# A long convolution and two MLP layers on one core: the work that GpSimd did behind the filter's first layer goes to VectorE

## The chip, the cores and the metric

The kernel runs on one core of a Trainium2 chip. The metric is device time in microseconds (us), measured around the whole program. The kernel before takes 1390.85 us, the median of three runs that lie between 1390.0 and 1391.01 us.

A core has five engines with a queue each: TensorE (PE, with the weight loads PEld beside it), VectorE (DVE), ScalarE (ACT), GpSimd (POOL) and SyncE (SP, here only for DMAs). An engine takes its instructions in the order of its queue. Matmul results land in PSUM; a tile of PSUM or SBUF that is used again has to be free first, and that is a wait as much as a missing operand is.

## The reference

```
h    = (relu(pos_emb @ w1) @ w2) * exp(-0.01*pos)      # filter, S=12480 x 128
y    = irfft(rfft(x*v, 2S) * rfft(h, 2S))[:S]          # long convolution
a    = x * y                                           # 12480 x 128
r    = relu(a @ moe_w_in)**2 @ moe_w_out               # 128 -> 2048 -> 128
h2   = r @ moe2_w_in
out  = (h2 * sigmoid(1.702*h2)) @ moe2_w_out           # 128 -> 2048 -> 128
```

All in fp32. The four weight matrices of the MLP come as 64-bit floats, which the kernel reads as pairs of 32-bit words (`raw`, low and high word side by side) and turns into two fp32r parts each, `hi` (rounded) and `lo` (the rest); each matmul of the MLP is three: hi*hi, hi*lo, lo*hi.

## The kernel before

**Stages.** The convolution is a Fourier transform of length 99 x 127 in two stages and back. Until 22 us the filter's first layer runs, until 87 us the first transform stage. From 87 to 227 us, `stage_s2` handles 99 frequencies in 50 pairs p: for each pair TensorE makes the spectrum `xk`, and of every fourth frequency on the filter's features `fk` and its spectrum `hk`; ScalarE copies `hk` to `hc`; VectorE makes the four partial products `t` (L357) of the complex product and the real half of `P` (L361, 128x256), GpSimd the imaginary half (L360); TensorE transforms back to `ob` (L369), ScalarE copies it into `A` (L371), and a DMA per four frequencies writes `A` to `bd` in DRAM. At the end the first columns of `bd` are read back transposed into `A` (`load_first`, L458).

**The boundary.** Between `stage_s2` and the MLP, `work.finish()` ends the weight conversions of the first MLP layer, and `sums_first` adds and subtracts halves of what was read back into `Gs` (L433 on VectorE, six times). With them TensorE makes tile 0 of the convolution's result (`yps`, L516); VectorE multiplies by x (L504 to L506, `hi`, `y`, `lo`). While it waits, TensorE repeats a matmul whose result nobody reads (`spare`, L645).

**The MLP.** 25 tiles of about 500 positions, 8 units a tile and layer. A unit is six matmuls in (`hin`) and, four units later (LAG), six out (`acc`). Layer 1 of the MLP on ACT: Relu (L588), Square (L589), and for every third of the first 40 units the rounding to `gh` (L591); on DVE that rounding else (L601, `gate`) and `gl = g - gh` (L612, `low`). The first 40 units (tiles 0 to 4) belong to layer 1 alone; from then on units of both layers alternate. For each later tile the sums of two rows of `bd` (`combine`, L433: 126 in all, 99x256) were GpSimd's, and so was a narrow rest of `y` (L532). The order per step n of the main loop: `work.tick(n)`, `unit_out` of n-4, `unit_in` of n, `high` of n-1, `gate` of n, `low` of n-1, then what the tile's own step brings: the loads at j=0, `front_rest` after j=2 of tile 0, `front_y` of the next tile after j=3, `front_x` after j=5.

**Weight conversions.** A chunk is 128x512 weights. `conversion` is a generator of ten steps; each tick advances it by one. Seven VectorE operations (L135 to L148) build the number in `cs` and `cm`, one tick each; then ScalarE rounds it to `hi` (L150), a tick without work, and VectorE makes `lo` (L152). Chunks 0 to 7 are done in `stage_s2` and `finish`, chunks 8 to 15 in the MLP from n=3 on, one every six steps.

**Names.** `uv` are rows of `bd` as loaded for sums, `b` and `Gs` hold sums, `yps` is the PSUM tile of the convolution's result, `yr` the kept rest columns, `xs` the columns of x.

Of the kernel before, what the change touches and what calls it, by code (L numbers as in the profile page):

```python
# [95 lines left out]
def conv_mlp_kernel(ctx: ExitStack, tc: tile.TileContext, xc, xt, vc, pt, w1, w2,  # L96
# [8 lines left out]
    ci2 = const.tile([N1, 2, N1], FP32, name="ci2")  # L105

# [18 lines left out]
    def conversion(n, raw, pool):  # L125
# [33 lines left out]
    class Weights:  # L159
# [60 lines left out]
    def filter_stage(fp, bank, h, inputs):  # L220
# [6 lines left out]
        nc.vector.memset(warm, 0.0)  # L227
        p_t = {}
# [76 lines left out]
    def stage_s2(sp, mp, A, w2b, hooks, work):  # L305
# [9 lines left out]
        with kp as kp, obp as obp:  # L315
# [14 lines left out]
            def filters(g):  # L330
# [10 lines left out]
                h_c[g] = sp.tile([128, FK, 2, D], FP32, tag="hc", name="hc", bufs=3)  # L341
# [39 lines left out]
            for p in range(NP + 2):  # L381
# [467 lines left out]
```

## Time and profile before

| | |
|---|---|
| median of three runs | 1390.85 us |
| the profiled execution | 1392.53 us, of which the span is 1390.7 us |
| TensorE busy in the span | 1377.2 us, 99% |
| VectorE, ScalarE, GpSimd busy | 1104.7, 949.6, 208.9 us |
| granted TensorE clock, mean | 0.998 of full speed |

How it is read: the span starts with the first and ends with the last instruction. A row of a timeline gives the start, the time that the row's instructions took together, engine, line, operation, output and inputs, and in brackets how long the engine sat idle before it and what ended that. [...] A row of a group by line gives the count, the busy time and the mean of one in ns, then the idle time before.

### The profile page before, as it was taken

How to read it: one execution, taken by the hardware profiler on the slowest of the kernel's cores; microseconds unless marked ns; L12 is line 12 of the kernel's file. 1: busy time of each engine (PE TensorE's matmuls, PEld its weight loads, DVE VectorE, ACT ScalarE, POOL GpSimd, SP SyncE). 2: the span in 40 equal slices, each digit the busy share in tenths (PEclk: the TensorE clock that was granted, in tenths of full speed). 3: DMA queues.
4: the chain of work that ended last, by engine and by line, in shares of the span. 5: the costliest groups of instructions: out<-in, count | busy, mean ns of one | idle time of the engine just before them, and what ended most of it. 6: DMA issues, size and time to landing. Idle time of an engine off the chain costs nothing.

```text
span 1390.7 us, 19236 instructions
## 1 busy us (share of the span) xinstructions
PE 1377.2 (99%) x7756; PEld 1143.1 (82%) x7756; DVE 1104.7 (79%) x1170; ACT 949.6 (68%) x1071; POOL 208.9 (15%) x208
## 2 busy tenths in 40 slices
PE   9999998999999999999999999999999999999998
PEld 8888885878788888888888888888888888888887
DVE  7559997888997777778777877777777777778887
ACT  2655553888776776667677776777677766777776
POOL 3013333522221011201121011111110120000000
PEclk9999999999999999999999999999999999999999
DMA  9967785212100001000010000100000100000000
GB/s 261 307 215 265 269 266 178 77 50 69 47 20 27 25 10 32 27 27 9 20 39 27 8 27 20 39 9 27 20 27 8 39 19 9 8 8 8 8 15 15
DMA packets 46583, 89.67 MB, mean 64 GB/s; under 512 B 4221, under 2 KB 31038, under 8 KB 45982
## 3 DMA queue, kind: packets, MB, share of 16 engines
q1 hardware_dynamic: 37427, 63.69, 15.1%
q10 hardware_dynamic: 9067, 24.75, 4.7%
q8 instruction: 61, 1.00, 0.3%
q14 instruction: 28, 0.23, 0.0%
HBM read 63.62 MB, written 24.81 MB: 64 GB/s over the span
## 4 chain that ended last, share of the span: by engine, by line
PE 79%; DVE 2%; ACT 2%; issue 0%; ACTq 0%
PE acc L560 13%; PE hin L560 13%; PE hin L561 13%; PE acc L561 13%; PE hin L562 12%; PE acc L562 12%; PE yps L516 3%; DVE gl L612 1%; ACT g L589 1%; ACT g L588 1%; DVE gh L601 0%; DVE g L603 0%; ACT gh L591 0%; DVE lo L493 0%; PE hin L578 0%
## 5 line engine op out<-in xcount | busy, mean ns | idle before, releaser
L612 DVE TENSOR_TENSOR gl<-g,gh 128x1004 fp32r<-128x1004 f32 (+4 forms) x400 | 493.6, 1234 | 33.8 <-ACT gh L608 33.6
L588 ACT ACTIVATE g<-hin 128x1004 f32<-128x1004 f32 (+4 forms) x200 | 201.1, 1005 | 226.9 <-PE hin L562 214.5
L560 PE MATMUL acc<-gh,w 128*128 128x502 f32 (+4 forms) x800 | 314.0, 392 | 2.4 <-DVE lo L493 2.4
L561 PE MATMUL acc<-gl,w 128*128 128x502 f32 (+4 forms) x800 | 312.1, 390 | 1.3 <-DVE gl L612 1.2
L562 PE MATMUL acc<-gh,w 128*128 128x502 f32 (+4 forms) x800 | 311.6, 390 | 0.0
L560 PE MATMUL hin<-hi,w 128*128 128x502 f32 (+4 forms) x798 | 311.3, 390 | 0.3 <-DVE g L603 0.3
L561 PE MATMUL hin<-lo,w 128*128 128x502 f32 (+4 forms) x798 | 311.0, 390 | 0.0
L562 PE MATMUL hin<-hi,w 128*128 128x502 f32 (+4 forms) x798 | 310.5, 389 | 0.0
L603 DVE TENSOR_TENSOR g<-hin,g 128x1004 f32<-128x1004 f32 (+4 forms) x200 | 238.6, 1193 | 46.6 <-ACT g L593 46.4
L601 DVE CAST gh<-g 128x1004 fp32r<-128x1004 f32 (+4 forms) x185 | 132.8, 718 | 152.0 <-ACT g L589 152.0
L593 ACT ACTIVATE g<-hin 128x1004 f32<-128x1004 f32 (+4 forms) x200 | 200.0, 1000 | 73.8 <-PE hin L562 65.8
L589 ACT ACTIVATE g<-g 128x1004 f32<-128x1004 f32 (+4 forms) x200 | 208.0, 1040 | 6.3
L608 ACT CAST gh<-g 128x1004 fp32r<-128x1004 f32 (+4 forms) x200 | 202.7, 1014 | 1.7 <-DVE g L603 1.7
L560 PEld LDWEIGHTS acc<-gh,w 128*128 128x128 f32 x800 | 150.9, 189 | 35.6 <-DVE lo L493 2.8
L560 PEld LDWEIGHTS hin<-hi,w 128*128 128x128 f32 x798 | 150.5, 189 | 34.8 <-ACT g L588 2.1
L561 PEld LDWEIGHTS acc<-gl,w 128*128 128x128 f32 x800 | 150.7, 188 | 31.9 <-DVE gl L612 2.5
L562 PEld LDWEIGHTS acc<-gh,w 128*128 128x128 f32 x800 | 150.7, 188 | 30.7
L562 PEld LDWEIGHTS hin<-hi,w 128*128 128x128 f32 x798 | 150.8, 189 | 30.4
L561 PEld LDWEIGHTS hin<-lo,w 128*128 128x128 f32 x798 | 150.9, 189 | 29.9
L433 POOL TENSOR_TENSOR Gs<-uv 99x256 f32<-99x256 f32 x82 | 91.8, 1149 | 442.2 <-DMA uv<-bd 367.2
L433 POOL TENSOR_TENSOR b<-uv 99x256 f32<-99x256 f32 x44 | 48.9, 1140 | 269.9 <-DMA uv<-bd 194.8
L360 POOL TENSOR_TENSOR P<-t 128x256 f32<-128x256 f32 (+1 forms) x50 | 48.1, 961 | 155.6 <-DVE t L357 139.2
(72 smaller groups left out, 1047.2 us busy)
## 6 DMA issues: line engine op xcount, KB each, us to landing
uv<-bd SPq DMA_DIRECT2D x64, 198.0 KB
m<-in_c_s_dram SPq DMA_DIRECT2D x49, 256.0 KB
bd<-A ACTq DMA_DIRECT2D x24, 512.0 KB
x<-in_xc_dram SPq DMA_DIRECT2D x16, 384.0 KB
v<-in_vc_dram SPq DMA_DIRECT2D x16, 384.0 KB
Gs<-gd ACTq DMA_DIRECT2D x10, 512.0 KB
raw<-in_moe_w_in_dram SPq DMA_DIRECT2D x8, 512.0 KB
raw<-in_moe_w_out_dram SPq DMA_DIRECT2D x8, 512.0 KB
```

The lines of the kernel that those rows point to most:

```text
L360: nc.gpsimd.tensor_tensor(out=P[:, 0:n, 1], in0=t[:, 0:n, 0, 1], in1=t[:, 0:n, 1, 0], op=ALU.add)
L433: engine.tensor_tensor(out=b[:, :, s, c], in0=uv[:, 0, :, c], in1=uv[:, 1, :, 1 - c], op=ALU.add if s != c else ALU.subtract)
L560: nc.tensor.matmul(out=out, lhsT=a, rhs=hl[0], start=first, stop=False)
L561: nc.tensor.matmul(out=out, lhsT=a, rhs=hl[1], start=False, stop=False)
L562: nc.tensor.matmul(out=out, lhsT=b, rhs=hl[0], start=False, stop=last)
L588: nc.scalar.activation(out=g, in_=ps, func=ACTF.Relu)
L589: nc.scalar.activation(out=g, in_=g, func=ACTF.Square)
L593: nc.scalar.activation(out=g, in_=ps, func=ACTF.Sigmoid, scale=1.702)
L601: nc.vector.tensor_copy(out=gh, in_=g)
L603: nc.vector.tensor_tensor(out=g, in0=ps, in1=g, op=ALU.mult)
L608: nc.scalar.copy(out=gh, in_=g)
L612: nc.vector.tensor_tensor(out=gl, in0=g, in1=gh.bitcast(FP32), op=ALU.subtract)
```

## The change

GpSimd keeps only the sums of the filter's first layer. In `stage_s2` the filter's spectrum is stored with a negated copy of its imaginary part in front (one more ScalarE operation for each group, L351), so that one VectorE operation on 128x512 (L370) makes both halves of `P`. The last pair but one writes to another PSUM tile, the last result is copied by VectorE, `hk` of the last group moves ahead by two steps, and both reads of `bd` at the end go through SyncE's queue. The conversions write into the raw words instead of a tile `cs`, in six steps; in `stage_s2` two of the eight VectorE operations become ScalarE activations; all eight chunks run there, from step 2 every six steps. In a conversion the last two VectorE operations and ScalarE's copy (L157) now come in one tick. In the MLP a `combine_two` (L455 or L457, 99x512) takes the place of two `combine`; the sums of a tile wait in a list, `pending`, and VectorE takes two off it at each of j=1, 2 and 3 of a unit of layer 1, ahead of `gate`. The conversions there start at n=4.

```diff
@@ conversion
-        yield vec.tensor_scalar(out=s, in0=high, scalar1=20, scalar2=0x7FF, ...)
-        yield vec.tensor_scalar(out=s, in0=s, scalar1=896.0, scalar2=1151.0, op0=ALU.max, op1=ALU.min)
-        yield vec.tensor_scalar(out=s, in0=s, scalar1=896.0, scalar2=float(1 << 23), ...)
-        yield vec.scalar_tensor_tensor(out=s, in0=high, scalar=-(1 << 31), in1=s, ...)
-        m = pool.tile([128, WC], I32, tag="cm", name="cm", bufs=2)
+        m = pool.tile([128, WC], I32, tag="cm", name="cm", bufs=1)
         f = m.bitcast(FP32)
-        yield vec.tensor_scalar(out=m, in0=high, ...)
+        vec.tensor_scalar(out=m, in0=high, ...)
         yield vec.scalar_tensor_tensor(out=f, in0=low.bitcast(U32), scalar=2.0 ** -32, in1=m, ...)
-        yield vec.scalar_tensor_tensor(out=f, in0=f, scalar=2.0 ** -20, in1=s.bitcast(FP32), ...)
+        vec.tensor_scalar(out=low, in0=high, scalar1=20, scalar2=0x7FF, ...)
+        if i < 2:
+            nc.scalar.activation(out=low.bitcast(FP32), in_=low, func=ACTF.Relu,
+                                 scale=-1.0, bias=edges[:, 0:1])
+            yield nc.scalar.activation(out=low, in_=low.bitcast(FP32), func=ACTF.Relu,
+                                       scale=-float(1 << 23), bias=edges[:, 1:2])
+            yield
+        else:
+            yield vec.tensor_scalar(out=low, in0=low, scalar1=896.0, scalar2=1151.0, ...)
+            yield vec.tensor_scalar(out=low, in0=low, scalar1=896.0, scalar2=float(1 << 23), ...)
+        vec.scalar_tensor_tensor(out=low, in0=high, scalar=-(1 << 31), in1=low, ...)
+        vec.scalar_tensor_tensor(out=f, in0=f, scalar=2.0 ** -20, in1=low.bitcast(FP32), ...)
         yield nc.scalar.copy(out=hi, in_=f)
         yield
         yield vec.tensor_tensor(out=lo, in0=f, in1=hi.bitcast(FP32), op=ALU.subtract)
@@ filters, product, back
-                nc.scalar.copy(out=h_c[g][:, 0:n], in_=hk[:, :, 0:n].rearrange("p c k d -> p k c d"))
+                nc.scalar.copy(out=hc[:, 0:n, 1:3], in_=hk[:, :, 0:n].rearrange("p c k d -> p k c d"))
+                nc.scalar.activation(out=hc[:, 0:n, 0], in_=hk[:, 1, 0:n], func=ACTF.Copy, scale=-1.0)
...
-                nc.gpsimd.tensor_tensor(out=P[:, 0:n, 1], in0=t[:, 0:n, 0, 1], in1=t[:, 0:n, 1, 0], op=ALU.add)
-                nc.vector.tensor_tensor(out=P[:, 0:n, 0], in0=t[:, 0:n, 0, 0], in1=t[:, 0:n, 1, 1],
-                                        op=ALU.subtract)
+                nc.vector.tensor_tensor(out=P[:, 0:n], in0=t[:, 0:n, 0], in1=t[:, 0:n, 1], op=ALU.add)
...
-                nc.scalar.copy(out=A[:, 2 * p:2 * p + n], in_=ob[:, 0:n])
+                (nc.vector.tensor_copy if p == NP - 1 else nc.scalar.copy)(
+                    out=A[:, 2 * p:2 * p + n], in_=ob[:, 0:n])
@@ stage_s2
-                if p < NP - 2:
+                if p < NP - 4:
                     work.tick(p)
@@ combine
+    def combine_two(k, op):
+        uv, b = b_t[k]
+        b = b.rearrange("n j s c d -> n j (s c) d")
+        u, v = uv[:, 0], uv[:, 1]
+        if op == ALU.add:
+            nc.vector.tensor_tensor(out=b[:, :, 1:3], in0=u[:, :, ::-1], in1=v, op=op)
+        else:
+            nc.vector.tensor_tensor(out=b[:, :, 0:4:3], in0=u, in1=v[:, :, ::-1], op=op)
+    def pend(k):
+        pending.extend((k, op) for op in (ALU.add, ALU.subtract))
+    def combine_next(n):
+        for i in range(min(n, len(pending))):
+            combine_two(*pending.pop(0))
@@ load_b, load_rest
-            for s in range(1 if k < KF else 2):
-                for c in range(2):
-                    combine(k, s, c, nc.gpsimd)
+            pend(k)
@@ front_y
-                nc.gpsimd.tensor_tensor(out=y[:, n:], in0=yr[:, at:at + m], in1=x[:, n:n + m], op=ALU.mult)
+                nc.vector.tensor_tensor(out=y[:, n:], in0=yr[:, at:at + m], in1=x[:, n:n + m], op=ALU.mult)
@@ main loop of the MLP
-        spare(8)
+        spare(6)
...
-        work = Weights([8, 12, 9, 13, 10, 14, 11, 15], 3, 6, 3, cp)
+        work = Weights([8, 12, 9, 13, 10, 14, 11, 15], 4, 6, 3, cp)
...
                 if prev:
                     high(prev)
+                if l == 0 and j in (1, 2, 3):
+                    combine_next(2)
                 gate(un)
@@ conversions of the first layer
-            work = Weights([0, 4, 1, 5, 2, 6, 3], 3, 6.5, 5, cp, [(46, 7)])
+            work = Weights([0, 4, 1, 5, 2, 6, 3, 7], 2, 6, 5, cp)
```

VectorE's queue from the last product of `stage_s2` to the first result of tile 0, before (`w0` is a weight tile, `cs` and `cm` the conversions' tiles):

```order
L357 TENSOR_TENSOR t_2229<-xk_2213,hc_2200 128x512
L361 TENSOR_TENSOR P_2231<-t_2229 128x128
L148 SCALAR_TENSOR_TENSOR cm_2172<-cm_2172,cs_2077 128x512
L135 TENSOR_SCALAR cs_2250<-raw_2174 128x512
L137 TENSOR_SCALAR cs_2250<-cs_2250 128x512
L138 TENSOR_SCALAR cs_2250<-cs_2250 128x512
L152 TENSOR_TENSOR w0_958<-cm_2172,w0_958 128x512
L140 SCALAR_TENSOR_TENSOR cs_2250<-raw_2174,cs_2250 128x512
L144 TENSOR_SCALAR cm_2257<-raw_2174 128x512
...
L433 TENSOR_TENSOR Gs_69<-A_535 99x2x128 x6
L504 TENSOR_TENSOR hi0_2327<-yps_2306,xs_2136 128x492
```

The same stretch after:

```order
L367 TENSOR_TENSOR t_2210<-xk_2195,hc_2159 128x512
L370 TENSOR_TENSOR P_2212<-t_2210 128x256
L381 COPY A_538<-ob_2214 128x256
L153 SCALAR_TENSOR_TENSOR raw_1990<-raw_1990 128x512
L155 SCALAR_TENSOR_TENSOR cm_2121<-cm_2121,raw_1990 128x512
L159 TENSOR_TENSOR w0_961<-cm_2121,w0_961 128x512
L455 TENSOR_TENSOR Gs_70<-A_538 99x2x256
L457 TENSOR_TENSOR Gs_70<-A_538 99x2x2x128
L446 TENSOR_TENSOR Gs_70<-A_538 99x2x128 x2
L534 TENSOR_TENSOR hi0_2293<-yps_2272,xs_2124 128x492
```

Ten operations of conversions stood between the last product and the sums (three are left out above); three stand there now, and the copy of the last `ob` ahead of them.

VectorE's queue in tile 0, before (numbers tell the tiles apart: `gl_2354` is unit 0, `gl_2381` unit 1):

```order
L601 CAST gh_2353<-g_2352 128x2x492
L612 TENSOR_TENSOR gl_2354<-g_2352,gh_2353 128x2x492
L601 CAST gh_2394<-g_2393 128x2x492
L612 TENSOR_TENSOR gl_2381<-g_2379,gh_2380 128x2x492
L552 COPY yr_2296<-yps_2400 128x196
```

And after (`uv_2301` are the rest's rows, `uv_2320` and `uv_2323` those for tile 1):

```order
L629 CAST gh_2313<-g_2312 128x2x492
L455 TENSOR_TENSOR b_2304<-uv_2301 99x2x256
L457 TENSOR_TENSOR b_2304<-uv_2301 99x2x2x128
L640 TENSOR_TENSOR gl_2314<-g_2312,gh_2313 128x2x492
L455 TENSOR_TENSOR Gs_70<-uv_2320 99x2x256
L457 TENSOR_TENSOR Gs_70<-uv_2320 99x2x2x128
L629 CAST gh_2352<-g_2351 128x2x492
L640 TENSOR_TENSOR gl_2337<-g_2335,gh_2336 128x2x492
L580 COPY yr_2264<-yps_2360 128x196
L455 TENSOR_TENSOR Gs_70<-uv_2323 99x2x256
L457 TENSOR_TENSOR Gs_70<-uv_2323 99x2x2x128
```

The sums that GpSimd made beside VectorE's queue now stand in it, and the last two stand behind the rounding of unit 2 (`gh_2352`) and the `gl` of unit 1.

VectorE's queue around the rounding copy of one weight chunk in the MLP, before:

```order
L601 CAST gh<-g 128x1008
L612 TENSOR_TENSOR gl<-g,gh 128x2x492
L148 SCALAR_TENSOR_TENSOR cm<-cm,cs 128x512
L135 TENSOR_SCALAR cs<-raw 128x512
L612 TENSOR_TENSOR gl<-g,gh 128x1008
L137 TENSOR_SCALAR cs<-cs 128x512
```

And after, at n=7:

```order
L629 CAST gh<-g 128x2x492
L640 TENSOR_TENSOR gl<-g,gh 128x2x492
L153 SCALAR_TENSOR_TENSOR raw<-raw 128x512
L155 SCALAR_TENSOR_TENSOR cm<-cm,raw 128x512
L640 TENSOR_TENSOR gl<-g,gh 128x2x492
```

with ScalarE's queue at the same place after:

```order
L616 ACTIVATE g<-hin 128x2x492
L617 ACTIVATE g<-g 128x2x492
L157 CAST w_2242<-cm 128x512
L616 ACTIVATE g<-hin 128x2x492
L617 ACTIVATE g<-g 128x2x492
```

Before, `cm` was finished (L148) one tick ahead of ScalarE's copy of it. Now L155 and the copy L157 belong to one tick, so that L157 stands right behind the Square of unit n-1 and ahead of the Relu of unit n, while the L155 that it reads stands on VectorE behind the rounding (L629) of unit n-1 and the `gl` of unit n-2.

## Rows read from the trace of the kernel before

**Rows 1.** The page, busy time of each engine in the whole span.
```profile
PE 1377.2 (99%) x7756; PEld 1143.1 (82%) x7756; DVE 1104.7 (79%) x1170; ACT 949.6 (68%) x1071; POOL 208.9 (15%) x208
```
**Rows 2.** Busy time by stage: `stage_s2`, tiles 0 to 4, steady state.
```profile
88.00:222.00 134.00, 133.78 (x977) 115.96 (x977) 123.34 (x150) 69.11 (x103) 45.73 (x48) 1.00 0.76 253
...
250.00:345.00 95.00, 94.30 (x524) 77.23 (x524) 81.36 (x105) 81.81 (x89) 28.55 (x28) 1.00 0.18 61
500.00:1200.00 700.00, 700.00 (x3546) 578.13 (x3546) 545.98 (x537) 502.15 (x538) 83.77 (x83) 1.00 0.07 22
```
**Rows 3.** Groups by line and shape in 88 to 222 us.
```profile
L342 ACT COPY hc<-hk 128x1024 f32<-128x1024 f32 x24 | 23.2, 1017 | 14.3 <-PE hk L340 12.9 <-DVE t L357 1.4
L361 DVE TENSOR_TENSOR P<-t 128x256 f32<-128x256 f32 x48 | 20.4, 425 | 4.9
L146 DVE SCALAR_TENSOR_TENSOR cm<-raw,cm 128x512 f32<-128x512 uint32 x7 | 8.5, 1218 | 0.0
```
**Rows 4.** Timeline of PE from the end of `stage_s2` to tile 0.
```profile
222.87 1.13 PE L369 MATMUL ob<-P,m 128*128 128x256 f32 x4 [0.41 <-POOL P L360]
224.72 1.10 PE L369 MATMUL ob<-P,m 128*128 128x256 f32 x4 [0.72 <-ACT A L371]
226.54 0.67 PE L369 MATMUL ob<-P,m 128*128 128x256 f32 x2 [0.72 <-issue]
227.05 6.76 PE L645 MATMUL spare<-xs,ci 99*99 99x492 f32 x16
235.24 1.73 PE L516 MATMUL yps<-ci,Gs 99*64 99x99 f32 x28 [1.42 <-DVE Gs L433]
...
239.16 2.49 PE L578 MATMUL hin<-hi,w 128*128 128x492 f32 x4
```
**Rows 5.** The boundary: timelines of ACT and DVE, and DMA's busy tenths from 224 to 236.
```profile
227.65 0.27 ACTq L374 DMA_DIRECT2D bd<-A  x1
234.76 2.62 DVE L433 TENSOR_TENSOR Gs<-A 99x256 f32<-99x256 f32 x6
DMA  0000299991000001000004797585000735789998
```
**Rows 6.** Tile 0: timelines of ACT and PE.
```profile
242.13 0.99 ACT L588 ACTIVATE g<-hin 128x984 f32<-128x984 f32 x1 [8.01 <-PE hin L578]
248.09 1.02 ACT L589 ACTIVATE g<-g 128x984 f32<-128x984 f32 x1
247.06 2.14 PE L516 MATMUL yps<-ci,Gs 99*64 99x99 f32 x40
```
**Rows 7.** Tiles 1 and 2: timelines of PE and DVE.
```profile
298.44 0.39 PE L560 MATMUL hin<-hi,w 128*128 128x502 f32 x1
309.43 0.39 PE L560 MATMUL hin<-hi,w 128*128 128x502 f32 x1
311.87 0.50 PE L561 MATMUL acc<-gl,w 128*128 128x502 f32 x1 [0.69 <-DVE gl L612]
295.00 0.68 DVE L601 CAST gh<-g 128x1004 fp32r<-128x1004 f32 x1 [0.58 <-ACT g L589]
295.60 1.20 DVE L612 TENSOR_TENSOR gl<-g,gh 128x1004 fp32r<-128x1004 f32 x1
296.71 0.42 DVE L144 TENSOR_SCALAR cm<-raw 128x512 int32<-128x512 int32 x1
299.93 0.68 DVE L146 SCALAR_TENSOR_TENSOR cm<-raw,cm 128x512 f32<-128x512 uint32 x1
310.08 1.74 DVE L612 TENSOR_TENSOR gl<-g,gh 128x1004 fp32r<-128x1004 f32 x1
```
**Rows 8.** Start of layer 2: timeline of PE, a stretch by busy time, timeline of ACT.
```profile
373.46 0.49 PE L560 MATMUL acc<-gh,w 128*128 128x492 f32 x1 [2.40 <-DVE lo L493]
374.50:377.90 3.40, 3.40 (x10) 2.77 (x9) 3.40 (x5) 1.01 (x1) 0.00 (x0) 0.50 0.00 0
399.59 0.62 ACT L150 CAST w<-cm 128x512 fp32r<-128x512 f32 x1 [2.10 <-DVE cm L148]
```

More of the change, by code (lines that the diff above doesn't have):

```diff
@@ L105, in conv_mlp_kernel @@
     ci2 = const.tile([N1, 2, N1], FP32, name="ci2")
+    edges = const.tile([128, 2], FP32, name="edges")
     bd = dram.tile([2, NJ, N1, 2, D], FP32, name="bd")
@@ L159, in conv_mlp_kernel, with __init__ @@
     class Weights:
-        def __init__(self, chunks, start, gap, lead, pool, rest=()):
+        def __init__(self, chunks, start, gap, lead, pool):
             self.pool, self.raw, self.run = pool, {}, []
-            self.plan = [(int(start + k * gap), n) for k, n in enumerate(chunks)]
-            self.fetches = [(at - lead, n) for at, n in self.plan] + [(at, n) for at, n in rest]
-            self.plan += [(1 << 30, n) for at, n in rest]
+            self.plan = [(start + k * gap, n) for k, n in enumerate(chunks)]
+            self.fetches = [(at - lead, n) for at, n in self.plan]
         def tick(self, i):
@@ L227, in filter_stage @@
         nc.vector.memset(warm, 0.0)
+        nc.vector.memset(edges[:, 0:1], 1151.0)
+        nc.vector.memset(edges[:, 1:2], float(255 << 23))
         p_t = {}
@@ L366, in back @@
                 n, m, P = pair(p), m_t.pop(p), P_t.pop(p)
-                ob = obp.tile([128, 2, 2, D], FP32, tag="ob", name="ob")
+                ob = (kp.tile([128, FK, D], FP32, tag="fk", name="ob", bufs=1).rearrange(
+                    "p (k c) d -> p k c d", c=2) if p == NP - 2 else
+                      obp.tile([128, 2, 2, D], FP32, tag="ob", name="ob"))
                 for j in range(n):
@@ L456, in load_first @@
         for h in range(2):
-            queue = nc.scalar if rows.stop == N1 and h else nc.sync
-            queue.dma_start(out=A[rows, h * JF1:(h + 1) * JF1],
-                            in_=bd[h, 0:JF1, rows].rearrange("j k c d -> k j c d"))
+            nc.sync.dma_start(out=A[rows, h * JF1:(h + 1) * JF1],
+                              in_=bd[h, 0:JF1, rows].rearrange("j k c d -> k j c d"))
         for h, k in late_h:
@@ L467, in sums_first @@
             b_t[k] = uv[:, :, k * JG:(k + 1) * JG], sums(bp, k)
-        for k, s in sorted({(j // JG, 0 if sign > 0 else 1) for j, sign, _, _ in whole(0)}):
-            for c in range(2):
-                combine(k, s, c, nc.vector)
+            need = {0 if sign > 0 else 1 for j, sign, _, _ in whole(0) if j // JG == k}
+            for n in range(2):
+                if len(need) == 2:
+                    combine_two(k, (ALU.add, ALU.subtract)[n])
+                else:
+                    combine(k, min(need), n)
         loaded[0] = KF - 1
@@ L544, in load_rest @@
             b_t[k] = uv, b
-            for s in range(2):
-                for c in range(2):
-                    combine(k, s, c, nc.gpsimd)
+            pend(k)
         def front_rest():
```

45 lines of the change are left out of this document (24 added, 21 removed).

## The prediction

> **What bounds the kernel now.** I read first the busy time on the page [rows 1]: TensorE works in 99% of the span, VectorE in 79%, GpSimd in 15%. Then the table by stage [rows 2]: from 500 to 1200 us TensorE is busy for 700.00 of 700, and in `stage_s2` for 133.78 of 134, though VectorE has 123.34 there. Work that moves between the other engines can be worth something only where TensorE stands still, and the reader should look for such places in TensorE's own timeline. [...] At the boundary between `stage_s2` and the MLP it idles in short pieces and fills the rest with matmuls that nobody reads [rows 4]. In tiles 0 to 4, where ScalarE has 81.81 and VectorE 81.36 of 95 us [rows 2], it waits once for a `gl` that took 1.74 us instead of 1.20 beside GpSimd [rows 7]. [...]
>
> **Steady state and `stage_s2`: 0 and +0.3.** From 400 us on GpSimd's sums come to VectorE, two or four operations of 99x512 a tile (126 sums, two at a time, over 24 tiles). I price each like the 128x512 one that stood alone, 0.68 us [rows 7], at most 2.7 us a tile, with the rest of `y` 3.1; of a tile's 44 us there (16 units at 2.75, below) VectorE's 545.98 of 700 [rows 2] leave it 22%, 9.7 us. TensorE was never kept waiting there, so nothing is gained either: 0. In `stage_s2` VectorE's `P` grows from 0.425 [rows 3] to 0.68 us, 48 times: +12 us. Against that, operations beside GpSimd took 1218 ns [rows 3] where 0.68 is the price alone [rows 7], and two of eight conversion steps go to ScalarE, so VectorE's 123.34 does not rise. The negated copy reads half of what the 1.017 us copy of `hc` reads [rows 3]; at 0.6 us, 24 times, it adds 14 us to ScalarE's 69.11 of 134 [rows 2]. The cover of both is TensorE's own 133.78. What is not covered is the first product, which now waits for two negated copies, and a first conversion one tick earlier: +0.3, between -0.5 and +1.5; if ScalarE became late at a fifth of a us for each of 24 groups, +4.8.
>
> **Boundary: -5.0.** Before, TensorE waited 0.41, 0.72 and 0.72 us ahead of the last three `ob` [rows 4]: for GpSimd's half of `P`, for the copy that frees the one PSUM tile, for the last pair. GpSimd is gone from this, pair 48 has another PSUM tile, and there are no conversion steps on VectorE among the last products; the two larger `P` cost 0.5. The last write, issued at 227.65 [rows 5], goes out 2.2 us earlier. What was read back landed between 230.3 and 232.4, the busy DMA slices of 0.3 us [rows 5]; I take 231.2, where the slices first fill. The sums began only at 234.76 [rows 5], since ten conversion operations stood ahead of them. Now three do, which fit into the wait for the DMA, so -3.5 more. Against it: both reads on one queue, +0.3, and the 512 KB write of the four frequencies before, which now has less head start, +0.3. The sums take 2 x 0.68 + 2 x 0.44 (a sixth of 2.62 us [rows 5]) = 2.2 us instead of 2.62, but the first `yps` needs both of the large ones, 1.4 us instead of 0.48 after their start (235.24 against 234.76): net +0.1. Sum -5.0, range -7 to -3. Twelve spares of 0.42 us (6.76 / 16 [rows 4]) end before the sums, as sixteen did.
>
> **Tile 0: +4.4.** Here the change adds a wait. GpSimd made these sums beside VectorE's queue, and `front_y` of tile 1 ran without waiting at 247.06 [rows 6]. Now the rest's sums follow the `gate` of unit 0 (Relu at 242.13 [rows 6], Square, then 0.6): they end near 246.1, and `front_rest`, due at about 244.7, waits 1.4 us. The last two sums stand behind `gate` of unit 2 and `gl` of unit 1. ScalarE's chain of three units ends at 248.09 + 1.02 = 249.1 [rows 6]; on VectorE follow 0.6 (`gate`), 1.1 (`gl`), 0.3 (`yr`) and 2 x 0.64: 252.4. Of the 2.14 us of `front_y(1)` [rows 6] three of five segments need those sums, 1.1 to 1.28 us, so the first `acc` starts near 253.5 instead of 249.2. Queued behind the sums are `gate` of unit 3 and `gl` of unit 2, which nobody needs for 5 us. +4.4, between +2 (if part of ScalarE's chain is ahead) and +5.
>
> **Clock: +0.8.** After an idle of 2.40 us the granted clock was 0.50 for 3.40 us [rows 8], which at half speed loses up to 1.7 us. Tile 0 gets such an idle; I take half of that loss, between 0 and 1.7. The spell that followed the boundary's idle of 1.42 us [rows 4] I leave as it is.
>
> **Copies of weights in tiles 0 to 4: +2.3.** A unit in and out lasts (309.43 - 298.44) / 4 = 2.75 us [rows 7]. ScalarE's copy of tick n now waits until VectorE has done `gate` of n-1 (0.59), `gl` of n-2 (1.11), and two steps (0.60 each), after the Square of n-1: 2.9 us; behind it stands the Relu of unit n, 2.8 us late. Such a wait is in the trace: ahead of the copy at 399.59 ScalarE did nothing for 2.10 us until VectorE had its `cm` [rows 8]. [...] By a queue that let the Relu pass, this term would be -0.7.
>
> TensorE bears some delay: `acc` of unit n comes three units (8.25 us) after its `hin`, and `gl` of n is ready one unit and 2.05 (Relu, Square) + 0.6 + 1.1 after it, 6.5 us: slack 1.75. So a copy costs about 1.0 us where nothing else helps, 1.25 where unit n also has its rounding on ScalarE. Six copies fall here, at n = 7, 13, 19, 25, 31, 37. At 13 and 37 the unit before is rounded on ScalarE, so VectorE doesn't wait for its Square: 0. At 19 and 25 a `front_y` (2.14 us [rows 6]) within the next three units covers the delay but for some carried over: 0.4 each. At 7 and 31 nothing covers it: 1.25 each. Sum 3.3; the old stall behind the 1.74 us `gl` goes (0.69 idle, with the restart 1.0 [rows 7]): +2.3. The least is -1 (ScalarE's 13 us of idle takes in all), the most +9 (1.5 us at each of six).
>
> Three steps of each chunk now write every second word of `raw`. No row has a strided write; a strided read takes 0.42 us, and an operation with two inputs 0.68 [rows 7], so a step costs 0 to 0.26 more, for 3 x 6 steps 4.7 us of VectorE in a stage where it has 13 idle; I take 0, by the nearer row. [...]
>
> **Start of layer 2: -0.6.** GpSimd no longer slows VectorE just before it (a 1218 ns operation for one of 0.68 [rows 3, 7], some four of them, 2.2 us), but three sums put 2.0 us into VectorE's queue there, and at tick 43 a copy stands ahead of ScalarE's rounding of `acc`, which `lo` needs. I leave the 2.40 us wait and its slow clock [rows 8], and take off 0.6 for the place at 399.59, where no copy is due any more. Between -5 (all of it gone) and +1.5.
>
> **Sum.** +0.3 - 5.0 + 4.4 + 0.8 + 2.3 - 0.6 = +2.2. The profiled execution took 1392.53 us, so 1394.7 in one like it; that execution was 1.7 above the median of 1390.85, and against the median the time is 1393.0.
>
> **Rivals.** A, the waits are taken in: ScalarE has 13 idle us in tiles 0 to 4 [rows 2], and after tile 0's idle it starts with nothing owed. Then no slow clock (0), copies -0.7, and without contention at layer 2 `lo` comes in time (2.40 + 1.6): 0.3 - 5.0 + 4.4 - 0.7 - 4.0 = -5.0, 1385.9. For it: one wait in 95 us before. Against it: that idle lies mostly in the yps gaps, and the copy still stands in line. Chance 0.27.
> B, slower: every wait of over 1 us is followed by a slow spell like that of [rows 8]. Two in tile 0, one each at 7 and 31: 4 x 1.6 - 0.8 = +5.6 on top, 1398.6. It decides from an idle of about 1.4 us on (the shortest before a slow stretch, at 235.24 [rows 4]). Against it: 0.72 and 0.69 us were not followed by one, and my waits at 7 and 31 are 1.25. Chance 0.20.
> C, ScalarE's added copies hold the products, so that `stage_s2` is no longer TensorE's: +4.8 instead of +0.3, 1397.5. Against it: 83 of 134 us after the change. Chance 0.05.
> The forecast has 0.48, on its own 1389 to 1396.5.
>
> **Range and chances.** 1384.5 to 1398.5 reaches into A on one side and to B on the other, leaving 0.1 on each. The measurement tells 0.2%, 2.8 us, from no change: faster is below 1388.07, slower above 1393.63. Faster: A 0.25 and 0.03 of the forecast, 0.28. Same: 0.28 of the forecast, 0.02 of A: 0.30. Slower: 0.17 of the forecast, B and C: 0.42.
>
> **What would show it.** The boundary: the first `hin` 5 us earlier against the start of `stage_s2`, the sums waiting for a DMA and not for a conversion. Tile 0: TensorE idle ahead of the two `yps` groups, released by VectorE's sums, and from first `hin` to first `acc` 14.4 us instead of 10. Copies: L157 idle about 2.9 us for VectorE at n=7 and 31, and `acc` waiting for L640 near it. Layer 2: the wait for `lo` near 370 us still there. I am wrong if TensorE shows no wait between tile 0 and layer 2 (A), if slow clock follows several waits (B), or if `stage_s2` is longer than 134 us for the same pairs (C).

## The result and the profile after

The changed kernel takes 1408.41 us, the median of four runs from 1406.93 to 1411.57; the kernel before took 1390.92 beside it. The ratio is 1.013, with a 95% interval of 1.0112 to 1.0148: slower by 17.5 us. The forecast was 1393.0, with a range that ended at 1398.5.

The profiled execution is the fastest of the four, 1406.93 us (span 1405.2). Where it lost 14.4 us against the profiled execution of before can be read by marking the same matmuls of TensorE in both traces (their starts, in us):

| event on TensorE | before | after | difference | gained or lost since the row above |
|---|---|---|---|---|
| first `xk`, start of `stage_s2` | 88.49 | 88.91 | +0.4 | +0.4 |
| last `ob`, its last matmul | 226.83 | 230.76 | +3.9 | +3.5 |
| first `hin`, tile 0 | 239.16 | 241.08 | +1.9 | -2.0 |
| first `acc`, tile 0 | 249.13 | 256.11 | +7.0 | +5.1 |
| tile 5's `yps`, its last matmul | 345.71 | 361.31 | +15.6 | +8.6 |
| tile 7's `yps`, its last matmul | 434.00 | 448.90 | +14.9 | -0.7 |
| last matmul | 1386.74 | 1401.12 | +14.4 | -0.5 |

Busy time by stage after, in the columns of [rows 2] (the stretch and its length, the busy time of PE, PEld, DVE, ACT and POOL with the number of instructions, the granted clock as a share of full speed, the share of the DMA engines, GB/s): GpSimd is at 0, the steady state is as before, and TensorE now stands still in `stage_s2` and in tiles 0 to 4.

```profile
88.00:222.00 134.00, 130.80 (x952) 112.63 (x954) 109.23 (x138) 88.56 (x140) 0.00 (x0) 1.00 0.74 245
250.00:345.00 95.00, 88.56 (x494) 70.98 (x494) 72.77 (x107) 71.33 (x78) 0.00 (x0) 0.96 0.20 68
500.00:1200.00 700.00, 700.00 (x3548) 578.14 (x3547) 553.11 (x589) 503.09 (x538) 0.00 (x0) 1.00 0.07 22
```

VectorE is busy for less time in both stages than in [rows 2] (109.23 for 123.34, 72.77 for 81.36, some 11% less, where the same stretches hold 3% and 6% fewer matmuls), and still TensorE is 3.2 and 6.4 us short. So it isn't VectorE's load that cost the time. ScalarE's load did rise in `stage_s2`, from 69.11 to 88.56 of 134 us.

**In `stage_s2`.** Timeline of ScalarE at one of four places that are alike (near 105, 139, 173 and 207 us), and of TensorE's `ob` there:

```profile
169.74 0.79 ACT L144 ACTIVATE raw<-raw,edges 128x512 f32<-128x512 int32 x1 [0.94 <-DVE t L367]
170.56 0.76 ACT L146 ACTIVATE raw<-raw,edges 128x512 int32<-128x512 f32 x1
171.22 0.99 ACT L350 COPY hc<-hk 128x1024 f32<-128x1024 f32 x1
172.12 0.59 ACT L351 ACTIVATE hc<-hk 128x512 f32<-128x512 f32 x1
172.60 1.01 ACT L350 COPY hc<-hk 128x1024 f32<-128x1024 f32 x1
173.50 0.61 ACT L351 ACTIVATE hc<-hk 128x512 f32<-128x512 f32 x1
173.98 0.60 ACT L381 COPY A<-ob 128x512 f32<-128x512 f32 x1
174.64 1.13 PE L379 MATMUL ob<-P,m 128*128 128x256 f32 x4 [0.80 <-ACT A L381]
```

Six operations in a row, 4.2 us, stand ahead of the copy that frees the one PSUM tile of `ob`, and TensorE waits for it. Conversions come every 6 pairs and `hk` every 4, so they meet every 12 pairs, about 33 us.

**At the boundary.** The last write goes out at 231.75 and the sums start 4.63 us later, released by the DMA and not by a conversion (ACT's queue, then DVE; the DMA that the trace names is the write, the wait is for the reads behind it, issued from 233.66 on):

```profile
231.75 0.27 ACTq L385 DMA_DIRECT2D bd<-A  x1
236.38 0.69 DVE L455 TENSOR_TENSOR Gs<-A 99x512 f32<-99x512 f32 x1 [2.01 <-DMA bd<-A]
```

**In tile 0.** Timeline of PE, and the last sum on DVE. Against [rows 6], `front_y` of tile 1 has a hole of 3.02 us in it. What follows the hole runs at half clock (granted clock 0.50 from 252.7 to 259.5 us): the last 24 matmuls of `yps` take 2.24 us where [rows 6] has 2.14 for all 40, and the `acc` after them has 0.41 us from one matmul to the next:

```profile
247.65 0.90 PE L546 MATMUL yps<-ci,b 99*64 99x98 f32 x16 [1.36 <-DVE b L457]
250.01 0.91 PE L546 MATMUL yps<-ci,Gs 99*64 99x99 f32 x16
253.94 2.24 PE L546 MATMUL yps<-ci,Gs 99*64 99x99 f32 x24 [3.02 <-DVE Gs L457]
256.11 0.78 PE L588 MATMUL acc<-gh,w 128*128 128x492 f32 x1
256.69 0.61 PE L589 MATMUL acc<-gl,w 128*128 128x492 f32 x1
253.20 0.69 DVE L457 TENSOR_TENSOR Gs<-uv 99x512 f32<-99x512 f32 x1
```

**In tiles 1 to 4 and at the start of layer 2.** Two rows of the waits from 250 to 400 us (engine, line and what it waited for; us in total, times, longest), then the longest of ScalarE's waits with what VectorE did before it, and TensorE's wait for `lo`:

```profile
ACT w L157 <- DVE cm L155: 21.6, 7, 4.5
PE acc L589 <- DVE gl L640: 4.5, 5, 1.0
```
```profile
306.46 0.68 DVE L455 TENSOR_TENSOR Gs<-uv 99x512 f32<-99x512 f32 x1
307.06 0.68 DVE L457 TENSOR_TENSOR Gs<-uv 99x512 f32<-99x512 f32 x1
307.66 0.68 DVE L629 CAST gh<-g 128x1004 fp32r<-128x1004 f32 x1
308.25 1.20 DVE L640 TENSOR_TENSOR gl<-g,gh 128x1004 fp32r<-128x1004 f32 x1
309.37 0.68 DVE L153 SCALAR_TENSOR_TENSOR raw<-raw 128x512 int32<-128x512 int32 x1
310.08 0.69 DVE L155 SCALAR_TENSOR_TENSOR cm<-cm,raw 128x512 f32<-128x512 f32 x1
310.81 0.62 ACT L157 CAST w<-cm 128x512 fp32r<-128x512 f32 x1 [4.46 <-DVE cm L155]
315.78 0.49 PE L589 MATMUL acc<-gl,w 128*128 128x502 f32 x1 [1.03 <-DVE gl L640]
390.52 0.49 PE L588 MATMUL acc<-gh,w 128*128 128x492 f32 x1 [3.22 <-DVE lo L523]
```

Each of the seven copies of a weight chunk in this stretch idles ScalarE, for 1.4 to 4.5 us. Behind five of them TensorE waits for `gl`, 4.5 to 7.5 us later; behind the one at 329.65 it doesn't. The wait for `lo` is 3.22 us where [rows 8] had 2.40, but here without a slow stretch behind it.

**From run to run** the mean granted clock of the changed kernel is 0.996, 0.995, 0.993 and 0.992, and the times rise in that order, 1406.93, 1407.97, 1408.85, 1411.57. The profiled run shows the least of this loss.

### The profile page after: what moved, and what is told of

Same layout as the page of the kernel before. It is cut to its first block, busy times and chain, and to the rows that moved or that the text cites. A ratio compares the mean times of both kernels' runs of the same rounds, so it can differ in the third digit from the quotient of the medians.

```text
span 1405.2 us, 18971 instructions
## 1 busy us (share of the span) xinstructions
PE 1379.8 (98%) x7752; PEld 1142.8 (81%) x7752; DVE 1099.4 (78%) x1240; ACT 970.6 (69%) x1111; POOL 12.7 (1%) x11
## 4 chain that ended last, share of the span: by engine, by line
PE 84%; DVE 7%; ACT 6%; issue 2%; DMA 1%; ACTq 0%; SPq 0%; DVEq 0%
PE acc L588 12%; PE acc L589 12%; PE acc L590 12%; PE hin L588 12%; PE hin L589 12%; PE hin L590 12%; PE s L286 5%; PE yps L546 3%; PE ob L379 2%; DVE gl L640 2%; PE xk L357 2%; ACT g L617 2%; ACT g L616 1%; PE fk L333 1%; ACT hc L350 1%
## 5 line engine op out<-in xcount | busy, mean ns | idle before, releaser
L640 DVE TENSOR_TENSOR gl<-g,gh 128x1004 fp32r<-128x1004 f32 (+4 forms) x400 | 477.1, 1193 | 31.7 <-ACT gh L636 31.6
L629 DVE CAST gh<-g 128x1004 fp32r<-128x1004 f32 (+4 forms) x185 | 125.6, 679 | 157.6 <-ACT g L617 157.2
L367 DVE TENSOR_TENSOR t<-xk,hc 128x1024 f32<-128x1024 f32 (+1 forms) x50 | 60.4, 1208 | 24.8 <-ACT hc L351 24.4
L379 PE MATMUL ob<-P,m 128*128 128x256 f32 x198 | 54.0, 396 | 3.9 <-ACT A L381 3.9
L357 PE MATMUL xk<-A,m 128*128 128x256 f32 x198 | 51.4, 382 | 0.1
```

The source lines that it names most:

```text
L357: nc.tensor.matmul(out=xk[:, j], lhsT=m[:, j, 0, :], rhs=A[:, 2 * p + j])
L379: nc.tensor.matmul(out=ob[:, j], lhsT=m[:, j, 1, :], rhs=P[:, j])
L629: nc.vector.tensor_copy(out=gh, in_=g)
L640: nc.vector.tensor_tensor(out=gl, in0=g, in1=gh.bitcast(FP32), op=ALU.subtract)
```

## The experiments

Theory Q: the loss is three places where a short operation stands in the wrong place of an in-order queue. Its rivals are named in each text. Ratios are against the kernel before, measured beside each run. Where an edit adds or removes lines, the line numbers behind it shift by up to four.

**One: the rounding copy a tick later.**

```diff
+        if i >= 2:
+            yield
         yield nc.scalar.copy(out=hi, in_=f)
```

> The changed kernel (1408.4 us), but in the conversions of the MLP ScalarE's rounding copy comes one tick after the two VectorE steps that make its input, as before the change. Theory Q (queues): ScalarE's copy, with the Relu behind it, waits for VectorE in the changed kernel (nine waits, 26.5 us in all in tiles 0 to 4 and the start of layer 2), and that is what keeps TensorE waiting there. Then the waits ahead of the copy go, the stalls of TensorE between 272 and 373 us (about 7 us) go, and the 3.2 us wait for lo near 387 shrinks below 2.4 us: 1398 to 1402 us. Rival V: VectorE itself, with the sums in its queue, is late with gl; the waits of ScalarE only mirror that, and a later copy gains under 2 us: 1406.5 to 1408.5 us.

Measured: 1394.25 us, ratio 1.0036 (1.0022 to 1.0049). ScalarE's waits for `cm` in that stretch fall from 21.6 us to this:

```profile
ACT w L159 <- DVE cm L155: 4.1, 3, 2.0
```

TensorE waits for no `gl` before 1387 us, and 1.62 instead of 3.22 us for `lo`. (The copy is L159 in this run.) From the `yps` of tile 1 to that of tile 5 the profile is 8.9 us shorter than the changed kernel's, some 0.9 of it because the half clock behind tile 0 ended sooner, and 2.6 more from there to tile 6's, around the start of layer 2: 11.4 in all, more than the 8 expected. Rival V is out: VectorE has the same work and is on time.

**Two: clamp and scale of the first layer's weights on VectorE.**

```diff
-        if i < 2:
+        if i < 0:
             nc.scalar.activation(out=low.bitcast(FP32), in_=low, func=ACTF.Relu,
```

> The changed kernel, but the conversions in the second transform stage clamp and scale on VectorE (two operations of about 0.42 us a chunk) instead of by two ScalarE activations of 0.77 us each. Theory Q: in the steps where the two activations stand ahead of two spectrum copies and two negated copies on ScalarE (near 105, 139, 173 and 207 us), the copy that frees the one PSUM tile of results comes late; without them those four stalls of 0.7 to 1.0 us go and the stage ends 3 to 3.5 us earlier: 1404.5 to 1406 us. Rival N: the negated copies alone are too much for that step; the stalls stay at 0.4 us or more and the gain is under 1 us: 1407.4 to 1408.5 us.

Measured: 1399.99 us, ratio 1.0071 (1.0056 to 1.0086). The last `ob` is at 226.17, 4.6 us earlier than after and 0.7 earlier than before. The negated copies are still there, and at the place near 139 us TensorE no longer waits (timelines of ACT and PE):

```profile
137.04 0.63 ACT L351 ACTIVATE hc<-hk 128x512 f32<-128x512 f32 x1
137.53 0.62 ACT L381 COPY A<-ob 128x512 f32<-128x512 f32 x1
138.25 1.08 PE L379 MATMUL ob<-P,m 128*128 128x256 f32 x4
```

So it was the two activations on top of the copies, not the copies alone (rival N). The edit takes away a load of ScalarE as well as the row of six operations; an edit that only moved the activations to another step was not run. Of the 8.4 us between the medians the profiles show 6.7; the rest comes from the changed kernel's other runs, which are slower than its profiled one.

**Three: tile 0's sums a unit earlier.**

```diff
-                if l == 0 and j in (1, 2, 3):
+                if l == 0 and j in ((1, 2, 3) if t else (0, 1, 2)):
```

> The changed kernel, but in tile 0 the three pairs of sums are taken off the list at units 0, 1 and 2 instead of 1, 2 and 3. Theory Q: the sums are late only because they stand behind the rounding of unit 2 and gl of unit 1; a unit earlier the rest's sums fit into the time in which VectorE waits for the first Square, and the last pair is done near 250 instead of 253.9 us. TensorE's waits of 1.36 and 3.02 us shrink to about 0 and under 1.5, and no stretch at half clock follows: first acc 4 to 5 us earlier, in all 5 to 6.5 us: 1402 to 1403.5 us. Rival D: the rows for the sums land too late for that (their loads stand behind other loads on SyncE's queue), and less than 2 us are won: 1406.5 to 1408.5 us.

Measured: 1402.55 us, ratio 1.0084 (1.0069 to 1.0099), 5.9 us less. Timeline of PE, without a wait in either group:

```profile
246.72 0.90 PE L546 MATMUL yps<-ci,b 99*64 99x98 f32 x16
249.09 2.11 PE L546 MATMUL yps<-ci,Gs 99*64 99x99 f32 x40
```

First `hin` to first `acc` takes 10.9 us instead of 15.0; the rows had landed in time.

**Four: all three edits.**

> The three edits of the runs before together. If the three places are independent, the gains add: 8 + 3.3 + 6 us off 1408.4, 1391 us (1388.5 to 1394), about the kernel before. Rival S (shared slack): what one place wins, another takes, since ScalarE and VectorE arrive at each tile with less lead: 1396 us or more.

Measured: 1383.74 us (1383.3 to 1384.66), ratio 0.9952 (0.9936 to 0.9969): 7 us faster than the kernel before, and the fastest kernel of this study. Rival S is out: the gains even exceed the sum that I had expected, though not the sum of the three measured ones (14.2 + 8.4 + 5.9 = 28.5, for 24.7 us). Tiles 0 to 4 are TensorE's again:

```profile
250.00:345.00 95.00, 95.00 (x543) 78.20 (x541) 83.04 (x121) 81.74 (x89) 0.00 (x0) 1.00 0.18 61
```

What is left of waits is 0.24 us ahead of the last `ob`, 1.60 ahead of the first `yps`, 0.45 in tile 0, 1.56 for `lo` and 0.55 at the very end, and the clock is 1.0 in every run.

**Five: in the kernel before, the sums ahead of the last conversions.**

```diff
-            work.finish()
+            for i in range(3):
+                work.tick(1 << 30)
             sums_first(bp, A)
...
-        spare(8)
+        spare(5)
         front_y(0)
+        first.finish()
```

> The kernel before (1390.9 us), with one thing of the change alone: at the boundary the sums of tile 0 stand ahead of the last six conversion operations on VectorE (which come after tile 0's first product), and five spares fill the time instead of eight. It shows when the rows that were read back had landed in the kernel before. Theory L1 (my step): landed at 231.2 us, 3.55 after the last write's issue; the sums start there, 3.5 us earlier than before, and the first hin 3 to 3.5 us earlier: 1387 to 1388 us. Theory L2: the changed kernel's sums waited until 4.6 us after that issue, so the same time, 232.3 us, holds here; the sums start 2.4 us earlier and the first hin about 2.4: 1388 to 1389 us. In both the rest of the run is as before.

Measured: 1394.37 us, ratio 1.0016 (1.0006 to 1.0027), not faster. Its purpose is met by the sums' row: they start at 232.08, 4.52 us after the last write's issue (227.56 here), which is L2. The first `hin` is 3.4 us earlier, more than L2 had: the sums also took 2.10 us instead of 2.62 [rows 5], and a second wait for them, 0.48 us at 237.44 in the kernel before, is gone. Then this edit makes a wait of its own, so that the times of both theories failed: ScalarE's last copy of a chunk (ACT), now late, stands ahead of the first Relu, while the `hin` that the Relu reads is ready since 238.2, and TensorE waits for the Relu (PE).

```profile
232.08 2.10 DVE L433 TENSOR_TENSOR Gs<-A 99x256 f32<-99x256 f32 x6 [5.16 <-DMA bd<-A]
237.48 0.71 PE L578 MATMUL hin<-lo,w 128*128 128x492 f32 x2 [0.53 <-DVE lo L506]
242.47 0.62 ACT L150 CAST w<-cm 128x512 fp32r<-128x512 f32 x1 [12.21 <-DVE cm L148]
242.99 0.98 ACT L588 ACTIVATE g<-hin 128x984 f32<-128x984 f32 x1
244.03 0.78 PE L560 MATMUL hin<-hi,w 128*128 128x492 f32 x1 [4.50 <-ACT g L588]
```

I had not counted that, and it is the same mechanism as in the change, in its plainest form.

**Six: all three edits, the MLP's sums on GpSimd.**

```diff
     def pend(k):
-        pending.extend((k, op) for op in (ALU.add, ALU.subtract))
+        for s in range(1 if k < KF else 2):
+            for c in range(2):
+                combine(k, s, c, nc.gpsimd)
```

> The kernel with all three edits (1383.7 us), but the sums of the MLP stage are GpSimd's again, four of 99x256 where VectorE had two of 99x512, right when their rows are loaded. It shows what the sums on VectorE are worth once they stand at the right place. Theory K (contention): GpSimd slows VectorE's operations of 0.68 us to about 1.22 while it works, which costs VectorE more than the sums do; in tiles 0 to 4 a stall of about 1 us comes back and the wait for lo at the start of layer 2 grows from 1.6 to 2.4 us or more, with a stretch at half clock: 1385 to 1388.5 us. Rival O (order only): what cost time was only where the sums stood, and GpSimd is as good a place: 1382.5 to 1384.5 us.

Measured: 1390.36 us, ratio 0.9984 (0.9973 to 0.9995), against 0.9952 with the sums on VectorE: rival O is out, the sums on VectorE are worth about 4.5 us at the right place. The price is not where Theory K had put most of it. In the profile 4.5 of 7.5 us are lost before the first `acc` (0.7 of them before `stage_s2` begins): GpSimd gets its rows at 244.01 and needs 4.19 us for four sums, for which TensorE waits four times, and a stretch at half clock begins among these waits (246.4 to 253.3). The waits at the start of layer 2 are 0.89 and 0.87 us, about as much as the 1.56 with VectorE.

```profile
244.01 4.19 POOL L448 TENSOR_TENSOR Gs<-uv 99x256 f32<-99x256 f32 x4 [2.04 <-DMA uv<-bd]
248.25 1.25 PE L550 MATMUL yps<-ci,Gs 99*64 99x98 f32 x12 [1.04 <-POOL Gs L448]
```

**Seven: all three edits, the product with GpSimd.** `P` is made as in the kernel before, and L351 is left out:

```diff
-                nc.vector.tensor_tensor(out=P[:, 0:n], in0=t[:, 0:n, 0], in1=t[:, 0:n, 1], op=ALU.add)
+                nc.gpsimd.tensor_tensor(out=P[:, 0:n, 1], in0=t[:, 0:n, 0, 1], in1=t[:, 0:n, 1, 0], op=ALU.add)
+                nc.vector.tensor_tensor(out=P[:, 0:n, 0], in0=t[:, 0:n, 0, 0], in1=t[:, 0:n, 1, 1],
+                                        op=ALU.subtract)
```

> The kernel with all three edits (1383.7 us), but the complex product is made as before the change: VectorE makes the real half of P, GpSimd the imaginary half, and ScalarE makes no negated copy. It shows what the whole product on VectorE is worth. TensorE sets the length of this stage in both, so only its end should move: before the change the last three results waited 0.41 to 0.72 us each, now 0.24 once. Theory E: 0.5 to 1.5 us slower, 1384.2 to 1385.2 us, from a wait for GpSimd's half near the end and conversions slowed by it. Rival Z: no difference within 0.4 us, since the last product's chain is as long with one VectorE operation of 0.69 as with 0.42 beside GpSimd's 0.97.

Measured: 1387.1 us, ratio 0.9962 (0.9949 to 0.9976), which overlaps that of all three edits: not told apart. The profile is 1.0 us longer, 1.1 of it at the first `hin`; TensorE waits for `t` at four places in the stage, which neither theory had; the first:

```profile
107.52 1.13 PE L358 MATMUL xk<-A,m 128*128 128x256 f32 x4 [0.44 <-DVE t L367]
```

**Eight: spares in the waits of tile 0.**

```diff
                     if t == 0 and j == 2:
+                        spare(1)
                         front_rest()
...
+                        if t == 0:
+                            spare(3)
                         front_y(t + 1)
```

> The changed kernel (1408.4 us), with matmuls that nobody reads put into TensorE's two waits of tile 0: one spare (0.83 us) ahead of the rest's convolution, three (2.5 us) ahead of tile 1's. The waits themselves stay. Theory H: the seven matmuls at 0.41 us after the wait of 3.02 us ran at half clock because TensorE had been idle; with the wait filled they run at 0.22, and 1.3 to 1.7 us are won in the profile, about 1406.5 to 1407.2 us. Rival P: the slow stretch is not tied to that wait (it follows from what came before, as the slow stretch at the boundary does in both kernels), and the time stays at 1408 to 1409 us.

Measured: 1404.66 us, ratio 1.0089 (1.0071 to 1.0107). The first `acc` after the filled wait runs at full clock (0.23 us from one matmul to the next) where the changed kernel had 0.41. The median is 3.8 us below the changed kernel's, more than Theory H had, and the two intervals of the ratio do not overlap. But the profiled run, the longest of its four, is no shorter than the changed kernel's: its slow stretch at the boundary is twice as long (6.8 for 3.4 us), and it has another one at the 3.23 us wait for `lo`, where the profile of the changed kernel had none. Rows by stretch, PEclk in the third column from the right: of this kernel after tile 0 and after `lo`,

```profile
255.50:259.50 4.00, 4.00 (x22) 3.35 (x19) 3.93 (x8) 0.97 (x1) 0.00 (x0) 1.00 0.29 92
388.50:394.00 5.50, 5.50 (x14) 4.45 (x15) 4.66 (x5) 3.14 (x5) 0.00 (x0) 0.50 0.02 3
```

and of the changed kernel at the same two places:

```profile
256.00:259.50 3.50, 3.50 (x12) 2.81 (x9) 3.21 (x6) 0.00 (x0) 0.00 (x0) 0.50 0.01 3
388.50:394.00 5.50, 3.48 (x16) 2.94 (x17) 4.13 (x6) 5.31 (x7) 0.00 (x0) 1.00 0.01 3
```

Theory H holds for the place that was filled. A wait of 3 us may or may not come with a slow stretch (3.23 us for `lo` here did, 3.22 in the changed kernel did not), and what decides it stays open.

**Nine: all three edits, conversions a unit earlier.** `Weights(..., 3, 6, 3, cp)` for `Weights(..., 4, 6, 3, cp)` in the MLP.

> The kernel with all three edits (1383.7 us), its conversions in the MLP started at unit 3 instead of 4, as before the change. In that kernel lo at the start of layer 2 still came 1.56 us late, behind the two steps L153 and L155 (1.3 us on VectorE) of the same unit; a unit earlier they stand ahead of that unit's sums. Theory Q: the wait for lo near 365 us shrinks to about 0.3 us and 1.2 to 1.7 us are won: 1382 to 1382.7 us. Rival B: VectorE is full there, so the steps push the rest back by as much wherever they stand, and nothing changes: 1383.3 to 1384.2 us.

Measured: 1386.2 us, ratio 0.9962 (0.995 to 0.9975), not faster than with all three edits alone; the median lies above the range of rival B too, but the intervals of the two ratios overlap. TensorE still waits 1.51 us for `lo`. VectorE is busy without a break through the whole of it, so the steps push the rest back wherever they stand (rival B):

```profile
366.07 0.69 DVE L155 SCALAR_TENSOR_TENSOR cm<-cm,raw 128x512 f32<-128x512 f32 x1
366.68 0.69 DVE L457 TENSOR_TENSOR Gs<-uv 99x512 f32<-99x512 f32 x1
367.28 0.68 DVE L459 TENSOR_TENSOR Gs<-uv 99x512 f32<-99x512 f32 x1
367.88 0.68 DVE L631 CAST gh<-g 128x1004 fp32r<-128x1004 f32 x1
368.48 1.18 DVE L642 TENSOR_TENSOR gl<-g,gh 128x984 fp32r<-128x984 f32 x1
369.57 0.67 DVE L525 TENSOR_TENSOR lo<-acc,hi 128x502 fp32r<-128x502 f32 x1
```

**Ten: the kernel before with the copy in the same tick.**

```diff
-        yield vec.scalar_tensor_tensor(out=f, in0=f, scalar=2.0 ** -20, in1=s.bitcast(FP32), ...)
+        vec.scalar_tensor_tensor(out=f, in0=f, scalar=2.0 ** -20, in1=s.bitcast(FP32), ...)
+        if i < 2:
+            yield
         yield nc.scalar.copy(out=hi, in_=f)
```

> The kernel before (1390.9 us), with one thing of the change alone: in the conversions of the MLP the last VectorE step and ScalarE's rounding copy of it come in one tick. The sums stay on GpSimd. Theory Q: the copy waits for gate of the unit before, a gl and one step on VectorE, and holds the Relu behind it, so waits of 2 to 4 us ahead of the copies appear on ScalarE, and TensorE loses 4 to 8 us between 265 and 400 us: 1395 to 1399 us. Rival V: the copy's wait hurts only where VectorE has the sums in its queue as well; without them under 2 us are lost: 1391 to 1393 us.

Measured: 1399.1 us, ratio 1.0059 (1.0045 to 1.0073): 8.1 us from one `yield`. Seven of the eight copies (L152 here) now idle ScalarE, 2.4 to 3.0 us each; the first:

```profile
267.64 0.63 ACT L152 CAST w<-cm 128x512 fp32r<-128x512 f32 x1 [2.44 <-DVE cm L148]
```

So the edit costs this much alone, with the sums still on GpSimd, and rival V is out. Not all of it need be the copies' own waits: the longest of TensorE's waits in this profile, 1.96 us at 277.87, comes behind a rounding of 3.35 us on VectorE beside GpSimd's sums (last section).

## Why the prediction was wrong

By its own steps, in the order of the sum (measured between the marked events of the two profiles):

| term | forecast | measured |
|---|---|---|
| start, `stage_s2` and boundary, to the first `hin` | +0.3 - 5.0 | +1.9 |
| tile 0, to the first `acc` | +4.4 | +5.1 |
| clock, copies, layer 2, to the end | +0.8 + 2.3 - 0.6 | +7.4 |

The profile is 14.4 us longer and not 2.2. Of the 12.2 us between, about 5.2 lie in `stage_s2`, 1.4 at the boundary, 1.5 in the clock and 4.2 in the copies. The forecast also took 1.7 us off, since the profiled run of before was that much above its median; the changed kernel's median is 1.5 us above its profile.

**`stage_s2`: wrong.** The step that failed is "The cover of both is TensorE's own 133.78". ScalarE's load of 83 of 134 us was a mean, and it left out the two activations of each conversion, which I had counted only as a relief of VectorE (11.6 us in this stretch; the load was 88.56). Four iterations had 4.2 us of work in a row ahead of the one copy that TensorE needs next. That is the effect of rival C, but its cause was put on 24 groups of copies instead of four meetings with a conversion, and its chance was 0.05. The four waits and a fifth of 0.21 make 3.1 us of idle; run two shows that they go with the activations, and the first `hin` then comes 5.2 us earlier (235.88 for 241.08).

**Boundary: right in kind, too large.** In run two, without the stalls of `stage_s2`, the first `hin` is 3.3 us earlier than before, where the first two terms had 4.7. Two terms were mis-sized. "I take 231.2" for the landing was 232.2 (run five: 4.52 us after the issue; after: 4.63), so 2.6 and not 3.5 us were to be had. The busy slices from 230.3 to 232.4 [rows 5] hold two writes of 180 KB too, issued behind the two reads of 44 KB, so they don't show when the reads were done. Of the 4.52 us of run five, 1.69 pass from the write's issue to that of the first read behind it (227.56 to 229.25), and 2.83 from there to the sums; after, it is 1.91 (231.75 to 233.66) and 2.72. I had 3.55 for both together. And the last write, forecast 2.2 us earlier, goes out 0.5 us earlier in run two (227.16 for 227.65); the waits that I named, 1.85 us, less the 0.5 for the larger `P` make 1.35 and not 2.2 to begin with.

**Tile 0: right**, place, releaser and size: the two waits are 1.36 + 3.02 = 4.4 us. The table has 0.7 us more because the last 24 matmuls of `yps` ran at half clock, which cost 1.0.

**Clock: too small.** The slow stretch behind the wait of 3.02 us cost about 2.3 us, counted on the same matmuls at both levels (1.0 up to the first `acc`, 1.3 behind it), where I had 0.8 and at most 1.7: it lasted 6.8 us, twice as long as that of [rows 8]. Rival B had the kind of loss, but its rule doesn't hold. From the boundary to the start of layer 2 TensorE waited over 1 us seven times (1.64, 1.36, 3.02, 1.03, 1.03, 1.04 and 3.22 us), and a slow stretch comes only with the 1.64 and the 3.02; in run four 1.60 and 1.56 us, both above its bound of 1.4, have none. What decides it stays open.

**Copies: the mechanism was right, the size off.** The step that failed is "Sum 3.3": by the starts of TensorE's matmuls the six copies cost 7.5 us. The copies at n = 7, 13, 19, 25, 31, 37 waited 3.31, 1.46, 4.46, 3.19, 4.03 and 1.42 us, where I had 2.9 at four and 0 at two, and cost TensorE 1.7, 0.9, 1.5, 0.3, 2.3 and 0.8 us, where I had 1.25, 0, 0.4, 0.4, 1.25 and 0. My chain held `gate`, a `gl` and the two steps alone. What else stands ahead of `gate` of unit n-1 on VectorE was missing: the two sums at n = 19 (1.2 us, the rows at 306.46 and 307.06 above), at 31 a `lo` and a conversion step; and at 13 VectorE came late from `y` and a `gl` to the two steps. `front_y` covered the copy at 25, as I had it, but not the one at 19. Run one takes most of these waits away, run ten makes such waits in the kernel before. That ScalarE's queue keeps its order, so that a waiting copy holds the Relu behind it, is what this term rested on; run five shows it: the `hin` is ready at 238.2, the Relu starts at 242.99 behind the copy, and TensorE waits 4.50 us.

**Start of layer 2: the size right by luck.** From tile 5 to tile 7 the table has -0.7 for my -0.6, but the parts are others: the wait for `lo` grew from 2.40 to 3.22 us, and the slow stretch that I had left in did not come. I had named the copy at n = 43 without a price; it waited 3.77 us, and with a later copy (run one) `lo` keeps TensorE waiting for only 1.62.

**Steady state: right.** From 480 us on the difference stays between 14.0 and 14.8. The strided writes (four steps a chunk, not three) cost nothing: L141 and L150 take 0.42 and 0.43 us, and L153, with two inputs, 0.68.

What the change was after is worth having: with the three places mended, the kernel beats the one before by 0.48%. Some 4.5 us are what the sums on VectorE gain over GpSimd (run six); the product on VectorE is not told apart from the old one (run seven).

## What to carry to other kernels

The mean load of an engine in a stage says little about a queue: where a short operation that somebody waits for shares a queue with bursts, count the longest row of operations ahead of it in one iteration, and where two periods meet (here 6 and 4 pairs: ScalarE had 88.56 of 134 us, and still four rows of 4.2 us made TensorE wait 0.51 to 0.80 us each).

An operation that only hands data on, as a rounding copy of a weight, should be issued one step after its input and not with it: standing ready, it costs its 0.6 us; waiting, it held everything behind it, for 1.4 to 4.5 us here.

When work moves from a spare engine into a busy one's queue, ask for each consumer what now stands ahead of it, and move it forward to where that engine idles; the same work a unit earlier was worth 6 us here.

## What the runs showed of the hardware

A VectorE operation beside GpSimd took far longer once than [rows 3] show, where it is 1218 ns for 0.68 us alone [rows 7]. In run ten a rounding of 0.68 us took 3.35 us, and ended 0.57 us after a row of eight sums of GpSimd (DVE, then POOL):

```profile
273.34 3.35 DVE L603 CAST gh<-g 128x1008 fp32r<-128x1008 f32 x1 [3.94 <-ACT g L591]
270.44 5.68 POOL L435 TENSOR_TENSOR Gs<-uv 99x256 f32<-99x256 f32 x8 [13.68 <-DMA uv<-bd]
```

It is a single operation: in the kernel before, the longest of the 185 of this line (L601) took 1.25 us, and in the changed kernel, whose GpSimd is idle in the MLP, 0.69 (L629). Why this one lasted over several of GpSimd's sums is not shown.

The granted clock is not the same from run to run of one kernel: 0.992 to 0.996 in the changed kernel, with waits of 3 us; 0.996 to 1.0 in the kernel before; 1.0 in all runs of the kernel with three edits, whose longest wait in the MLP is 1.6 us. But run nine, with 1.51 us for `lo` in its profile, has runs of 0.997 as well as 1.0, so the length of a wait alone does not decide it. The changed kernel's times rise as its clock falls, and its profile, the fastest run, shows the least of that; that its waits are what lowers the clock is likely, but not shown.
